# First batch's attention in two halves of 384 tokens, with a carried state column, and the order of all engine queues from a table of numbers

## The chip, the cores and the metric

The kernel runs on one core of one Trainium2 chip. The metric is the device time of one execution in microseconds (us): the median over runs is 608.11 us (three runs, 608.09 to 608.78). Engines are named as in the profile: PE (TensorE matmul), PEld (its weight load), DVE (VectorE), ACT (ScalarE), POOL (GpSimd), SP (the queue that issues the DMAs).

## What is computed

Three layers, one after another, for B = 4 batches, H = 8 heads, S = 768 tokens, D = 48 per head, so 384 channels. The first is a recurrent attention per head with a state of 48x48:

```python
f = 1.0 / (1.0 + np.exp(-f_logit))
for t in range(S):
    state = f[:, :, t, :, None] * state + np.einsum('bhd,bhe->bhde', k[:, :, t], v[:, :, t])
    y[:, :, t] = np.einsum('bhd,bhde->bhe', q[:, :, t], state)
```

Its output x (B, S, 384) goes through the second layer and that one's output through the third:

```python
theta = x @ w_theta
y = np.einsum('ts,bsd->btd', w_tok_r, x * np.cos(theta)) + np.einsum('ts,bsd->btd', w_tok_i, x * np.sin(theta))
u = x + y
x = u + np.maximum(u @ w_ch, 0.0)

h = np.maximum(x @ w_in, 0.0)
u, v = h[..., :512], h[..., 512:]
v_n = (v - mean(v)) / np.sqrt(var(v) + 1e-06)
v_s = np.einsum('ts,bsd->btd', w_spatial, v_n) + b_spatial[None, :, None]
out = (u * v_s) @ w_out
```

## The kernel before

**Stages.** Attention and second layer of all four batches form one long first part (up to about 345 us in the profile); the third layer of the four batches is the second part. In the first part PE works on the token mix of one batch (`p1_acc`, tiles `acc<-tk,z`, then `p1_h`, tiles `hh`), and the attention and angles of the next batch are laid between its matmuls. Batch 0 has no batch before it, so its attention and angles stand alone at the start of the program. That stretch is what the change rewrites.

**Attention.** The 768 tokens are 12 chunks of 64. Channels are packed densely: one dense group `g` holds 128 of the 384 channels of a batch, three groups per batch. `dense(b, g)` loads f, k, q of a group (each 128x768), forms exp and 1+exp on ACT, a running product inside each chunk on DVE (a scan, `icp<-f,one`), its log and exp on ACT (`cw`), and scales k and q on DVE (`k<-k,icp`, `icp<-cw,icp`, `cw<-icp,cw`, `q<-q,cw`). Twelve extra columns of k get the decay over a whole chunk, on POOL. In batch 0 group 0 alone is already cut in two halves of 384 tokens (`HALVES`, `cuts`). A *pair* `u` is two heads; there are four pairs a batch, and the fourth pair's channels are gathered out of the three groups by DMA into the tiles `kp` and `qp` (`att_gap`). For each pair: transposes of k (`att_k`, `pt<-ident,k`, copied by ACT to `kt`), the outer products k v of all chunks (`att_w`, `pw`, 24 matmuls), ACT copies of them and of the chunk decays, one DVE scan over 48x12 columns (`cu<-cu`, or `st`, `cb`) that turns them into the state after every chunk, the scores inside chunks (`att_s`, `psc`, 12 matmuls for six chunks, masked on DVE into `sc`), and the output (`att_x`, `px`, 46 matmuls: state times q from the second chunk on, and scores times v), copied by ACT to X.

**Second layer.** For each of six blocks of 128 tokens: transpose of X (`pt<-ident,X`), theta (`pth`), a range reduction on ACT and DVE (`sn`), two sines on ACT (another activation table than exp and log), and z = x cos, x sin on DVE. The token weights arrive as doubles, twelve parts `tok`, each turned to float32 on ACT and DVE (`tk<-ws`); a part feeds six `acc` matmuls. The theta weights (`ft<-ws`) and the channel weights w_ch (`wb<-ws`, `wc`) are converted in the same way. For batch 0 `acc`, `pth` and all attention matmuls take float32 operands, and one matmul is two rows of the trace.

**What sets the order.** Engine wrappers record every instruction of the first part (so the profile puts nearly all on one line, L496). `Plan.run` makes the order of each of the five queues (PE, DVE, ACT, POOL, SP) with a list scheduler that has a cost for each instruction, then repeats it with changed priorities drawn from the numbers in `STEPS`, and ties the instructions of each queue together in that order. POOL keeps program order, and `tables` keeps all instructions that need an activation table in program order. At the start PE runs `FILL` = 25 multiplications of the identity with itself, whose results nobody reads.

```python
self.act(f, f, AF.Exp, scale=-1.0)
A.activation(f, f, AF.Copy, bias=1.0)
V.reciprocal(fs[:, c], fc[:, :, 0])
V.memset(fc[:, :, 0:1], 0.0)
V.tensor_tensor_scan(icp, f, one, 0.0, op0=ALU.mult, op1=ALU.add)
```

Of the kernel before, what the change touches and what calls it, by code (L numbers as in the profile page):

```python
# [12 lines left out]
F32 = mybir.dt.float32  # L13
# [10 lines left out]
P = 128  # L24
# [24 lines left out]

WTICK, IDLE = 37, 25  # L50

FILL = 25

NEAR = 6
WARM = {}
# [8 lines left out]
SIGN = 0x80000000  # L64
REBIAS = 2.0**-112

MODE, HOP, ISSUE, RATE, NARROW, LAND, SLACK = 0.1, 0.11, 0.6, 310e3, 160e3, 1.2, 0.05
LEAD = 1.5  # L70
ROUNDS = 4
STEPS = [
# [11 lines left out]
]  # L84
HALVES = {0: 2}
SAMPLES, STALL, STEADY = 10, (0.07, 1.0, 3.0), 0.8
GLUE = 4
# [29 lines left out]
class Plan:  # L117
    def __init__(self, tc):
        self.tc, self.on, self.ops, self.tag, self.size = tc, True, [], {}, {}
        self.hist, self.table, self.blk, self.pri, self.gate, self.pool, self.first, self.idle = {}, None, 0, None, {}, None, {}, 0  # L120
# [4 lines left out]

    def cost(self, o, e, ins, out, src):
        n = max([b.n for b in out + src] or [0])
        k = type(ins).__name__
        if e == "A":
            if k == "InstActivation":  # L130
                return 0.19 + 0.84e-3 * n + (0.95e-3 * n if out[0].step > 2 and n > P else 0)
            return 1.28
        if e == "V":
            if o.name.startswith("tensor_tensor_scan"):
                return 0.16 + 2.07e-3 * n
            if o.name == "tensor_scalar":
                return 0.15 + 0.53e-3 * n
            if o.name == "reciprocal":
                return 0.22
            return 0.15 + 1.045e-3 * n  # L140
        if e == "G":
            return 0.1 + 0.8e-3 * n if o.name == "memset" else 0.8
        if e == "Q":
            return ISSUE
        m, r = out[0].rows, out[0].n
        o.mode = (src[-1].rows, m)
        if o.name == "transpose":
            return 0.109
        if len(src) == 2 and src[0].t == src[1].t:
            return 0.0  # L150
        if src[0].dt == F32R:
            return max(r / 2.4 + 13.3, m / 1.2 + 2) / 1e3
        if m < P:
            o.quad = (src[-1].p[0], out[0].p[0])
            return 0.064 + (0.05 if src[0].step > 1 else 0)
        return max(2 * (2 * r / 2.4 + 2), 214) / 1e3

    def add(self, e, name, ins):
# [4 lines left out]
        o.cost, o.mode = 0, None  # L163
        o.cost = self.cost(o, e, ins, o.out, o.src)
        o.bytes = max([b.n * b.rows * 4 for b in o.out] or [0])
        o.rate = RATE if max([b.rows for b in o.out] or [P]) > 96 else NARROW
# [19 lines left out]
        if e == "G":  # L186
            if self.pool is not None:
                o.dep.add(self.pool)
            self.pool = o
# [8 lines left out]
    def tables(self, o, func):  # L198
        o.func = func
        if self.table is not None:  # L200
            o.dep.add(self.table)
        self.table = o

    def prepare(self):
        ops = self.ops
        self.use, first = {}, set()
        for o in ops:
            o.new = []
            for b in o.out + o.src:
                if b.t in self.tag:  # L210
                    self.use.setdefault(b.t, set()).add(o)
                    if b.t not in first:
                        first.add(b.t)
                        o.new.append(b.t)
        self.order, self.units, self.succ, unit = {}, [], {}, {}
        for o in ops:
            for t in o.new:
                self.order.setdefault(self.tag[t], []).append(t)
# [7 lines left out]
        for u in self.units:  # L226
            mine, need = set(u), {}
            deps = {d for o in u for d in o.dep if d not in mine}
            u[0].deps = [(d, d.e == u[0].e and d.e != "Q") for d in sorted(deps, key=lambda d: d.i)]
            for o in u:  # L230
                for x in o.new:
                    need.setdefault(self.tag[x], []).append(x)
            u[0].need = list(need.items())
            for d, _ in u[0].deps:
                self.succ.setdefault(d, []).append(u)
            u[0].touch = {x for o in u for x in {b.t for b in o.out + o.src} if x in self.use}

    def schedule(self):
        free = {k: [(0.0, "")] * n for k, n in self.size.items()}
        self.took = []  # L240
        turn = {k: 0 for k in self.order}
        left = {t: len(s) for t, s in self.use.items()}
# [3 lines left out]
        for u in self.units:  # L246
            if not u[0].deps:
                insort(queue[u[0].e], (u[0].pri, u[0].i, 0.0, u))
# [1274 lines left out]
```

## Time and profile before

| | |
|---|---|
| median of three runs | 608.11 us |
| the profiled execution: its time, its span | 606.65 us, 604.9 us |
| PE busy in the span | 579.1 us (96%), 5704 matmul rows |
| DVE busy | 452.9 us (75%) |
| ACT busy | 349.3 us (58%) |
| POOL busy | 20.0 us (3%) |
| DMA, mean over the span | 230 GB/s, 139.42 MB |
| mean granted clock of PE | 0.983 |

The profiled execution is 1.75 us longer than its span (what lies around the first and last instruction) and 1.46 us shorter than the median. A granted clock of 1.00 is 2.4 GHz, one of 0.50 is 1.2 GHz; a value between is a stretch that holds both. Busy time of PE is taken from modelled ends, so a busy PE need not be PE at its peak; the distance of matmul starts tells more.

### The profile page before, as it was taken

Reading aid. Unit: us, or ns where it says so; the run is one execution under the profiler, and the core shown is the slowest. Engines: PE = TensorE matmul, PEld = TensorE weight load, DVE = VectorE, ACT = ScalarE, POOL = GpSimd, SP = SyncE. Lnnn points to the kernel's source line nnn. Section 1 sums busy time; section 2 is a strip of 40 time slices with the busy share of each in tenths; the row PEclk is TensorE's granted clock in tenths of the full one; section 3 lists DMA queues with packets and bytes.
Section 4 is the critical chain, followed back from the end, with each engine's and each line's share of the span. In section 5 each row is a group of like instructions: output and inputs, shape, how many; then the busy total and the mean of one; then the engine's idle time right before and its main releaser. Section 6 shows DMA issues by size and latency. Waiting matters only on the chain.

```text
span 604.9 us, 13976 instructions
## 1 busy us (share of the span) xinstructions
PE 579.1 (96%) x5704; PEld 533.0 (88%) x5704; DVE 452.9 (75%) x812; ACT 349.3 (58%) x649; POOL 20.0 (3%) x55
## 2 busy tenths in 40 slices
PE   7678998999999999999999999999999999999995
PEld 7675566877998999999999988999999999999995
DVE  5897899877898669857988269896668666957681
ACT  6757887478877699757973035534443454344421
POOL 3000010010010000000000000000000000000000
PEclk9589999999999999999999999999999999999998
DMA  8776779983689989667989899596029603940422
GB/s 301 226 221 221 224 251 286 322 280 124 234 280 285 314 279 298 203 214 246 298 305 317 312 313 350 199 376 233 28 93 360 231 21 110 376 154 15 138 97 84
DMA packets 65079, 139.42 MB, mean 230 GB/s; under 512 B 6128, under 2 KB 35312, under 8 KB 65008
## 3 DMA queue, kind: packets, MB, share of 16 engines
q1 hardware_dynamic: 65008, 138.45, 67.9%
q8 instruction: 47, 0.77, 0.6%
q14 instruction: 24, 0.20, 0.1%
HBM read 104.20 MB, written 31.85 MB: 225 GB/s over the span
## 4 chain that ended last, share of the span: by engine, by line
PE 80%; DMA 7%; DVE 6%; ACT 4%; issue 1%; SPq 0%; ACTq 0%; DVEq 0%
PE acc L496 24%; PE pg L496 12%; PE pu L496 8%; PE pv L496 8%; PE po L496 7%; PE hh L496 6%; PE pth L496 5%; DMA ws<-tok_dram 4%; PE psc L496 3%; PE px L496 3%; PE pw L496 2%; PE pt L496 2%; DMA xs<-x2d 1%; ACT sn L496 1%; DMA q<-qd_dram 1%
## 5 line engine op out<-in xcount | busy, mean ns | idle before, releaser
L496 PE MATMUL acc<-tk,z 128*128 128x384 f32 x792 | 172.1, 368 | 0.9 <-issue 0.9
L496 PEld LDWEIGHTS acc<-tk,z 128*128 128x128 f32 x792 | 138.0, 188 | 16.6 <-issue 0.8
L496 PE MATMUL pg<-sp,vn 128*128 128x384 f32 x504 | 88.0, 336 | 0.0
L496 PEld LDWEIGHTS pg<-sp,vn 128*128 128x128 f32 x504 | 87.4, 188 | 0.0
L496 PE MATMUL po<-wo,gt 128*128 128x384 f32 x288 | 52.1, 338 | 0.3 <-ACT gt L496 0.3
L496 PEld LDWEIGHTS po<-wo,gt 128*128 128x128 f32 x288 | 50.8, 188 | 0.8 <-ACT gt L496 0.6
L496 PE MATMUL pu<-x,wi 128*128 128x384 f32 x288 | 50.7, 335 | 0.0
L496 PEld LDWEIGHTS pu<-x,wi 128*128 128x128 f32 x288 | 50.1, 188 | 0.3
L496 PE MATMUL pv<-wi,x 128*128 128x512 f32 x216 | 50.4, 390 | 0.0
L496 PEld LDWEIGHTS pv<-wi,x 128*128 128x128 f32 x216 | 40.5, 188 | 8.1
L496 PE MATMUL hh<-uT,wc 128*128 128x384 f32 x216 | 41.7, 342 | 0.6 <-DVE uT L496 0.2
L496 PEld LDWEIGHTS hh<-uT,wc 128*128 128x128 f32 x216 | 37.9, 188 | 2.1 <-DVE uT L496 1.2
L496 ACT ACTIVATE gt<-g 128x384 fp32r<-128x384 f32 x32 | 16.7, 522 | 38.3 <-DVE g L496 38.2
L496 DVE TENSOR_TENSOR vn<-vr,vn 128x768 fp32r<-128x768 f32 x24 | 22.9, 956 | 19.8 <-ACT vn L496 19.0
L496 DVE BATCH_NORM_STATS2 st<-vr 128x6 f32<-128x512 f32 x24 | 16.4, 690 | 25.6 <-ACT vr L496 25.6
L496 PE MATMUL pth<-wh,xT 128*128 128x384 f32 x108 | 32.6, 356 | 0.0
L496 ACT ACTIVATE vn<-vr 128x768 fp32r<-128x768 f32 x24 | 20.3, 845 | 19.4 <-PE pg L496 18.8
L496 PE MATMUL psc<-qp,k 64*64 64x64 f32 x576 | 22.9, 234 | 8.1 <-ACT qp L496 6.0
L496 ACT ACTIVATE ws<-ws 128x768 f32<-128x768 f32 (+2 forms) x28 | 20.8, 741 | 16.9 <-DMA ws<-tok_dram 12.5
L496 PEld LDWEIGHTS psc<-qp,k 64*64 64x64 f32 x576 | 20.7, 147 | 9.6 <-ACT qp L496 6.4
L496 PE MATMUL px<-vc,sc 64*64 64x48 f32 x768 | 28.5, 228 | 0.0
L496 ACT ACTIVATE oo<-po 128x384 f32<-128x384 f32 x24 | 11.8, 492 | 25.5 <-PE po L496 21.3
(133 smaller groups left out, 1037.0 us busy)
## 6 DMA issues: line engine op xcount, KB each, us to landing
sp<-wpd SPq DMA_DIRECT2D x56, 576.0 KB, 6.3
tk<-tkp SPq DMA_DIRECT2D x48, 384.0 KB, 4.5
ws<-tok_dram SPq DMA_DIRECT2D x12, 768.0 KB, 6.4
tkp<-tk SPq DMA_DIRECT2D x24, 384.0 KB, 4.6
vn<-vu_dram SPq DMA_DIRECT2D x16, 288.0 KB, 4.6
vc<-va_dram SPq DMA_DIRECT2D x16, 288.0 KB, 4.7
tkd<-tk SPq DMA_DIRECT2D x12, 384.0 KB, 7.1
x2d<-xt SPq DMA_DIRECT2D x24, 192.0 KB, 3.9
```

The lines of the kernel that those rows point to most:

```text
L496: r = f(*a, **k)
```

## The change

**Halves.** In batch 0 every dense group now runs in two halves of 384 tokens (`half`), and so does everything behind it for each of the four pairs: transposes (`half_k`), gathers of the fourth pair (`half_gap`), loads of v (`half_load`), outer products and state scan (`half_w`), output (`half_x`). The program first does half 0 of all groups and pairs, then half 1. k has room for six extra columns behind each half. The state scan of a half has 48x7 columns instead of 48x12 for all: in half 0 a zero column closes each row; in half 1 the first column is the state at the end of half 0, which POOL keeps in `carry` (`carry<-cu`, `cu<-carry`). The angles of blocks 0 to 2 stand before the first dense group of batch 1, those of blocks 3 to 5 behind it. `MEMSET f` goes from DVE to POOL in every dense group. The conversion of w_ch moves from the start into the first mix (ticks `WCS` = 7, 9, 11). `FILL` is 16 instead of 25.

**Order.** The planner with its costs is gone. `LINE` gives for each engine the order of all units (a unit is one instruction; on PE one group of matmuls), 1614 numbers in all. POOL no longer has to keep program order. `tables` asks for order only between changes of the table, and `run` puts a table load in front of the exp and log instructions after each sine; the program holds 17 table loads instead of 13.

```diff
-HALVES = {0: 2}
+WCS = [7, 9, 11]
-FILL = 25
+FILL = 16
+LINE = {
+    "T": [
+        45, 61, 46, 47, 82, 48, 49, 50, 51, 52, 53, 54, 55, 56, 57, 58, 59, 60, 95, 91, 100, 120, 131, 127, 142, 136, 146, 151, 160, 156, 165, 185,
...
     def tables(self, o, func):
         o.func = func
-        if self.table is not None:
-            o.dep.add(self.table)
-        self.table = o
+        if self.table != func:
+            self.table, self.old, self.cur = func, self.cur, []
+        o.dep.update(self.old + self.cur[:1])
+        self.cur.append(o)
...
+        for e, l in LINE.items():
+            seq = [o for i in l for o in self.units[i]]
...
+                if e == "A" and o.func not in (None, func):
+                    func = o.func
+                    if func == "exp":
+                        ins.append(load().ins)
+                ins.append(o.ins)
+            for x, y in zip(ins, ins[1:]):
+                self.tc.add_manual_dep(y, x.name, no, reason="plan")
...
+    def decay(self, n, f, k, q, icp, cw, fs, cs):
+        self.act(f, f, AF.Exp, scale=-1.0)
+        A.activation(f, f, AF.Copy, bias=1.0)
+        V.reciprocal(fs, fc[:, :, 0])
+        G.memset(fc[:, :, 0:1], 0.0)
+        V.tensor_tensor_scan(icp, f, self.one[:, cs].rearrange("p c t -> p (c t)"), 0.0, op0=ALU.mult, op1=ALU.add)
...
+    def half(self, n, h):
+        for x, c in (("f", p), ("k", slice(kp.start, kp.stop - 6)), ("q", p)):
+            self.Q.dma_start(out=t[x][:, c], in_=self.a[x + "d"][n][:, p])
+        yield from self.decay(n, t["f"][:, p], k, t["q"][:, p], icp, cw, fs, slice(6 * h, 6 * h + 6))
+        if h == 0:
+            G.tensor_tensor(cx[:, 0:5], ce[:, 0:5], fs[:, 1:6], op=ALU.mult)
+            G.tensor_copy(cx[:, 5:6], ce[:, 5:6])
+        else:
+            G.tensor_copy(cx[:, 0:1], fs[:, 0:1])
+            G.tensor_tensor(cx[:, 1:6], ce[:, 0:5], fs[:, 1:6], op=ALU.mult)
...
+    def half_w(self, u, h):
+        G.memset(cu[:, 0 : 2 - h, :, 6:7], 0.0)
+        A.activation(cb[:, :, 0:6], K[:, None, TH:].to_broadcast([P, D, 6]), AF.Copy)
+        for n in range(3):
+            for s, i in ((0, 0), (1, 1), (1, 0), (0, 1)):
+                self.outer(w[s][64 * i : 64 * i + 64, n], u, 3 * h + n, s, i)
+        if h:
+            G.tensor_copy(ub[:, :, 0:1], self.carry[:, u, :, None])
+        for s in range(2):
+            A.activation(ub[:, :, h + s : h + s + 5 : 2], w[s].rearrange("p n e -> p e n"), AF.Copy)
+        V.tensor_tensor_scan(fl(cb), fl(ub), fl(cb), 0.0, op0=ALU.add, op1=ALU.mult)
+        if h == 0:
+            G.tensor_copy(self.carry[:, u, :, None], cb[:, :, 5:6])
...
+        for h in range(2):
+            for g in range(3):
+                run(self.half(g, h))
...
+                self.half_k(g, h)
+                self.half_gap(g, h)
+                if g:
+                    self.half_att(g - 1, h, X[0])
+            for u in (2, 3):
+                self.half_att(u, h, X[0])
+        run(self.p1_thetas(0, X[0], 0, 3))
+        run(self.ahead(self.dense(1, 0), 1000))
+        run(self.p1_thetas(0, X[0], 3, 6))
```

**What the order becomes, at three places.** The first is the head of the PE queue. `pt<-ident` is the fill, `pt<-ident,k_...` the transposes of a dense group's k, `pw` the outer products and `psc` the scores of pair 0. Before:

```order
L496 MATMUL pt<-ident 128x128 x25
L496 MATMUL psc<-qp_105,k_138 64x64 x12
L496 MATMUL pt<-ident,k_138 128x128 x6
L496 MATMUL psc<-qp_105,k_138 64x64 x12
L496 MATMUL pw<-vn_100,kt 64x48 x24
```

and now:

```order
L258 MATMUL pt<-ident 128x128
L258 MATMUL pt<-ident,k_137 128x128 x3
L258 MATMUL pt<-ident 128x128 x2
L258 MATMUL pt<-ident,k_203 128x128 x3
L258 MATMUL pt<-ident 128x128 x13
L258 MATMUL pw<-vn_100,kt 64x48 x12
L258 MATMUL psc<-qp_105,k_137 64x64 x12
```

Thirteen of the fills now stand behind the transposes of the second group (`k_203`) and ahead of pair 0's first outer products and scores.

The second place is DVE up to the masked scores `sc_108` of pair 0, which wait for those `psc`. Before, from the second scan of group 0 on (`k_138`, `q_141` are its k and q, `f_232` is group 1's f):

```order
L496 SCALAR_TENSOR_TENSOR icp<-f_135,one 128x384
L496 TENSOR_TENSOR k_138<-k_138,icp 128x384
L496 TENSOR_TENSOR sc_108<-psc,mask 128x384
L496 TENSOR_TENSOR icp<-cw,icp 128x384
L496 SCALAR_TENSOR_TENSOR cw<-icp,cw 128x384
L496 TENSOR_TENSOR q_141<-q_141,cw 128x384
```

and now (`f_202`, `f_296` are groups 1 and 2, `cu_249` is pair 0's state):

```order
L258 TENSOR_TENSOR q_138<-q_138,cw 128x384
L258 SCALAR_TENSOR_TENSOR icp<-f_296,one 128x384
L258 TENSOR_TENSOR icp<-cw,icp 128x384
L258 SCALAR_TENSOR_TENSOR cw<-icp,cw 128x384
L258 RECIPROCAL fs_205<-f_202 128x6
L258 TENSOR_TENSOR sc_108<-psc,mask 128x384
L258 SCALAR_TENSOR_TENSOR cu_249<-cu_249 128x336
L258 TENSOR_TENSOR q_204<-q_204,cw 128x384
```

The first halves of three groups are begun before pair 0's scores, and group 1's q and all that follows stand behind `sc_108`.

The third place is PE where the token mix begins. `ft` are the theta weights, `tk_900` and `tk_979` the first part of the token weights, `z_788` and `z_873` the first block of z, `k_748` batch 1's first k. Before:

```order
L496 MATMUL psc<-qp_105,k_748 64x64 x24
L496 MATMUL pth<-ft_171,xt 128x384
L496 MATMUL pth<-ft_178,xt 128x384
L496 MATMUL pth<-ft_185,xt 128x384
L496 MATMUL pt<-ident,X_132 128x128 x3
L496 MATMUL pth<-ft_171,xt 128x384
L496 MATMUL pth<-ft_178,xt 128x384
L496 MATMUL pth<-ft_185,xt 128x384
L496 MATMUL acc<-tk_900,z_788 128x384 x2
```

and now (`cu_738`, `cu_803` are the states of pairs 2 and 3 in half 1):

```order
L258 MATMUL px<-vc_102,sc_108 64x48 x4
L258 MATMUL psc<-qp_107,kp 64x64 x12
L258 MATMUL pth<-ft_157,xt 128x384
L258 MATMUL pth<-ft_164,xt 128x384
L258 MATMUL pth<-ft_171,xt 128x384
L258 MATMUL pw<-vn_101,kt 64x48 x12
L258 MATMUL acc<-tk_979,z_873 128x384 x2
L258 MATMUL acc<-tk_987,z_890 128x384 x2
L258 MATMUL acc<-tk_979,z_873 128x384 x2
L258 MATMUL px<-cu_803,qp_107 64x48 x4
```

Transposes, outer products and scores of batch 1's first pair (`k_748`) no longer stand ahead of the first `acc`; the last output of batch 0 (`px<-cu_803`) stands behind it.

## Rows read from the trace of the kernel before

**Rows 1.** The page: busy time by engine, and PE and its granted clock in 40 slices.

```profile
span 604.9 us, 13976 instructions
PE 579.1 (96%) x5704; PEld 533.0 (88%) x5704; DVE 452.9 (75%) x812; ACT 349.3 (58%) x649; POOL 20.0 (3%) x55
PE   7678998999999999999999999999999999999995
PEclk9589999999999999999999999999999999999998
```

**Rows 2.** Busy time by stage: stretch, its length, busy us (instructions) per engine, clock, DMA share, GB/s.

```profile
4.37:60.62 56.25, 41.99 (x939) 36.73 (x938) 46.41 (x75) 38.29 (x74) 4.51 (x15) 0.85 0.78 251
60.62:109.73 49.11, 47.08 (x593) 31.06 (x592) 44.31 (x61) 38.31 (x67) 3.17 (x6) 1.00 0.82 259
110.83:345.00 234.17, 233.22 (x2784) 219.37 (x2784) 180.24 (x269) 163.54 (x287) 8.80 (x19) 1.00 0.80 268
345.00:604.90 259.90, 252.81 (x1378) 242.29 (x1376) 180.73 (x407) 106.48 (x219) 0.00 (x0) 0.99 0.54 188
```

**Rows 3.** PE in order of time: start, length, what, count [idle before <-releaser].

```profile
1.51 5.49 PE L496 MATMUL pt<-ident 128*128 128x128 f32 x24 [1.51 <-POOL ident masks.py:199]
6.58 3.55 PE L496 MATMUL pt<-ident 128*128 128x128 f32 x27
...
24.68 1.53 PE L496 MATMUL pw<-vn,kt 64*64 64x48 f32 x48 [0.96 <-ACT kt L496]
26.00 2.42 PE L496 MATMUL psc<-qp,k 64*64 64x64 f32 x48
...
49.60 0.94 PE L496 MATMUL pw<-vn,kt 64*64 64x48 f32 x48 [0.24 <-ACT kt L496]
50.48 2.20 PE L496 MATMUL pth<-ft,xt 128*128 128x384 f32 x6
...
52.94 1.61 PE L496 MATMUL psc<-qp,k 64*64 64x64 f32 x48
...
61.31 1.45 PE L496 MATMUL acc<-tk,z 128*128 128x384 f32 x4
...
71.64 11.77 PE L496 MATMUL acc<-tk,z 128*128 128x384 f32 x36
83.25 0.82 PE L496 MATMUL pt<-ident,k 128*128 128x128 f32 x6
```

**Rows 4.** DVE in order of time: the first instructions, one of each size, and the last.

```profile
4.37 0.19 DVE L496 RECIPROCAL fs<-f 128x6 f32<-128x6 f32 x1 [0.89 <-ACT f L496]
4.73 0.96 DVE L496 TENSOR_TENSOR_SCAN icp<-f,one 128x384 f32<-128x384 f32 x1
12.45 0.56 DVE L496 SCALAR_TENSOR_TENSOR cw<-icp,cw 128x384 f32<-128x384 f32 x1
13.92 1.76 DVE L496 TENSOR_TENSOR_SCAN icp<-f,one 128x768 f32<-128x768 f32 x1
16.38 0.95 DVE L496 TENSOR_TENSOR k<-k,icp 128x768 f32<-128x768 f32 x1
17.95 1.36 DVE L496 TENSOR_TENSOR_SCAN cu<-cu 128x576 f32<-128x576 f32 x1 [0.62 <-ACT cu L496]
57.13 1.95 DVE L496 SCALAR_TENSOR_TENSOR tk<-ws,tk 128x768 uint32<-128x768 uint32 x2
59.66 0.96 DVE L496 TENSOR_TENSOR z<-sn,X 128x768 f32<-128x768 f32 x1
109.17 0.56 DVE L496 TENSOR_TENSOR uT<-xt,uT 128x384 fp32r<-128x384 f32 x1 [1.06 <-ACT uT L496]
```

**Rows 5.** The chain of waits in order of time, up to 130 us: start, length, what.

```profile
19.45 2.80 PE px L496 x92
...
30.99 4.69 DMA qp<-q
...
107.81 1.53 PE px L496 x92
109.34 1.49 PE acc L496 x4
110.83 3.15 PE hh L496 x18
```

**Rows 6.** DMA issues of the first 50 us: count, size of one, median us from issue to landing.

```profile
k<-kd_dram SPq DMA_DIRECT2D x5, 384.0 KB, 6.3
k<-kd_dram SPq DMA_DIRECT2D x2, 192.0 KB, 5.3
kp<-k SPq DMA_DIRECT2D x2, 97.5 KB, 4.7
kp<-k SPq DMA_DIRECT2D x2, 48.8 KB, 2.7
```

**Rows 7.** Busy time and clock (the last three figures: clock, DMA share, GB/s) of single stretches.

```profile
16.00:26.00 10.00, 6.69 (x188) 6.03 (x182) 9.20 (x13) 7.55 (x15) 1.08 (x3) 0.50 0.74 204
36.00:60.00 24.00, 19.43 (x484) 15.85 (x485) 18.41 (x30) 17.05 (x37) 0.49 (x3) 1.00 0.67 206
```

More of the change, by code (lines that the diff above doesn't have):

```diff
@@ L124, in tile @@
             self.tag[t.name], self.size[key] = key, bufs
[L126 to L156, printed above, removed]
     def add(self, e, name, ins):
@@ L199, in tables @@
         o.func = func
-        if self.table is not None:
-            o.dep.add(self.table)
-        self.table = o
+        if self.table != func:
+            self.table, self.old, self.cur = func, self.cur, []
+        o.dep.update(self.old + self.cur[:1])
+        self.cur.append(o)
     def prepare(self):
[L205 to L218, printed above, removed]
+        self.units, unit = [], {}
+        for o in self.ops:
             if o.e == "T" and o.blk in unit:
@@ L225, in prepare @@
             self.units.append(u)
[L226 to L236, printed above, removed]
@@ L543, in ln_exp @@
         self.ready = True
-        self.table(self.A.preload_act_table_set("natural_log_exp_and_others"), "exp")
+        if not self.plan.on:
+            self.table(self.A.preload_act_table_set(TABLES), "exp")
     def group(self):
@@ L586, in mm1 @@
             self.T.matmul(out, lhsT=l, rhs=r, start=(i == 0), stop=(i == n - 1))
-    def warm(self, p, key):
-        for _ in range(WARM.get(key, 0)):
-            self.T.matmul(p[:, 0:P], lhsT=self.ident, rhs=self.ident, start=True, stop=True)
     def att_open(self, ctx):
@@ new lines, in part, with half_k @@
+    def part(self, h):
+        return slice((TH + 6) * h, (TH + 6) * h + TH + 6)
+    def half_k(self, g, h):
+        self.group()
+        k = self.dn[g]["k"][:, self.part(h)]
+        p = self.bank("pt")
+        for i in range(3):
+            self.T.transpose(p[:, P * i : P * i + P], k[:, P * i : P * i + P], self.ident)
+        kt = self.KT[:, 0 : NT * DM].rearrange("p (n d) -> p n d", n=NT)
+        self.A.activation(kt[:, 3 * h : 3 * h + 3, P * g : P * g + P], p[:, 0:DM].rearrange("p (n d) -> p n d", n=3), AF.Copy)
@@ new lines, in half_x @@
+    def half_x(self, u, h, X):
+        self.group()
+        A, T, pr = self.A, self.T, u % NP
+        Q, sc, v, st = self.att_kq(u)[1], self.SC[u % 2], self.VC[u % 2], self.st[u, h]
+        ps = [self.bank("px")[:, 0 : 3 * D].rearrange("p (n d) -> p n d", n=3) for _ in range(2)]
+        for n in range(3 * h, 3 * h + 3):
+            four = [(c, i, ps[i][64 * (c % 2) : 64 * (c % 2) + 64, n - 3 * h]) for c in (2 * n, 2 * n + 1) for i in range(2)]
+            for c, i, o in four:
+                r = slice(64 * i, 64 * i + 64)
+                if c:
+                    T.matmul(o, lhsT=Q[r, C * c : C * c + C], rhs=st[r, c - 6 if h else c - 1], start=True, stop=False)
+            for c, i, o in four:
+                r = slice(64 * i, 64 * i + 64)
+                T.matmul(o, lhsT=sc[r, C * c : C * c + C], rhs=v[r, c], start=(c == 0), stop=True)
+        for i in range(2):
+            o = 2 * D * pr + D * i
+            A.activation(X[:, 3 * h : 3 * h + 3, o : o + D], ps[i], AF.Copy)
@@ new lines, in half_att, with outer @@
+    def half_att(self, u, h, X):
+        self.half_load(u, h)
+        if u < 3:
+            self.att_mask(u, h)
+        self.att_s(u, h)
+        self.half_w(u, h)
+        self.half_x(u, h, X)
+    def outer(self, out, u, n, s, i):
+        r = slice(64 * s, 64 * s + 64)
+        if u % NP < 3:
+            o, step = DM * n + P * (u % NP) + C * i, 1
+        else:
+            o, step = DM * n + STEP * D * i + STEP - 1, STEP
+        self.T.matmul(out, lhsT=self.KT[r, o : o + (C - 1) * step + 1 : step], rhs=self.VN[u % 2][r, i, n], start=True, stop=True)
@@ L883, in p1_tok, with p1_thetas @@
         return [x.rearrange("p (s t) -> p s t", s=2) for x in t]
-    def p1_thetas(self, b, X):
-        terms = self.p1_xt(b, X, 0)
-        for tb in range(NT):
-            nxt = self.p1_xt(b, X, tb + 1) if tb + 1 < NT else None
+    def p1_thetas(self, b, X, first=0, last=NT):
+        terms = self.p1_xt(b, X, first)
+        for tb in range(first, last):
+            nxt = self.p1_xt(b, X, tb + 1) if tb + 1 < last else None
             self.p1_z(b, X, tb, self.p1_theta(b, tb, terms))
@@ L1416, in run @@
         self.mixes(X, sa, sw, se)
-        self.plan.run()
+        self.plan.run(lambda: self.A.preload_act_table_set(TABLES))
+        self.last, self.ready = self.plan.end, False
         self.ln_exp()
```

448 lines of the change are left out of this document (96 added, 352 removed), and 77 rows, old and new, of tables (LINE, STEPS).

## Prediction

> **What bounds the kernel now.** I read the page first [rows 1]: PE is busy in 96% of the span, its slices (15 us each) are nearly full from the fifth on, and the granted clock falls below 0.9 in the second and third alone. So the question is where PE does not yet run full. The busy times by stage [rows 2] answer it. From 110.83 to 345.00 us PE is busy 233.22 of 234.17 us, so what a new order can take out of the long middle is about 1 us; the last stretch, 259.9 us, is outside the table. What is left is the start. PE in order of time [rows 3] shows the first token-mix matmul (`acc`) at 61.31 us: until then batch 0's attention runs alone, as a chain PE, ACT, DVE, PE. DVE is the busiest engine beside PE there: 46.41 of 56.25 us up to the first z and 44.31 of 49.11 us from there to the third uT, the operand of the first `hh` [rows 2, 4], which starts at 110.83 [rows 5]. Its idle time is 9.8 and 4.8 us, 14.6 together. So up to 110 us DVE's queue sets the pace, and I account for the change on DVE, then test the result against PE.
>
> **DVE up to the first z.** Sizes from [rows 4]: products 0.56 (384 columns) or 0.95 (768), product scans 0.96 or 1.76, state scan 1.36 (576 columns), two steps of a token part 1.95. A state scan of 336 columns has no row; from 0.96 and 1.76 a column costs 0.8/384 = 2.1 ns, so it takes 0.86, between 0.79 (336/576 of 1.36) and 0.96. Reciprocals, memsets and the one-step conversions of 0.36 or 0.56 come from the same view. In the order of the program, before: scans 2x0.96 + 3x1.76 = 7.2; state scans 4x1.36 = 5.4; score masks 10x0.56 = 5.6; products 8x0.56 + 12x0.95 = 15.9; theta weights 4.4; channel weights 5.6; one token part 2.5; the rest 3.1; together 49.7. Now: scans 6x0.96 + 1.76 = 7.5; state scans 7x0.86 = 6.0; masks 7x0.56 = 3.9; products 24x0.56 = 13.4; theta weights 4.4; two token parts 4.9; the rest 3.7; together 43.9. The channel weights and most of batch 1's first group are no longer ahead of z, a second token part and two angles are.
>
> **DVE from there to the third uT.** Before 47.3: seven token parts 17.2, five z 4.8, eight products 7.6, scans 3.5, state scans 4.1, the rest 10.1. Now 56.1: five token parts 12.3, five z 4.8, twelve products 11.4, scans 5.3, state scans 4.9, the postponed channel weights 5.6, the rest 11.8. Over both pieces: 96.9 before, 100.0 now. Halves cost 3.1 us of DVE, since every cut instruction pays its fixed part twice; `MEMSET f`, 0.07 each, is the only thing taken off. The record shows 46.4 + 44.3 = 90.7 busy for the 96.9, because neighbours overlap: a factor of 0.94. The 3.1 becomes 2.9.
>
> **The sum.** DVE begins at 4.37 in both, since both begin with the same half of group 0. Let X be DVE's idle time up to the third uT: 14.6 before. The first `hh` then comes 14.6 - 2.9 - X = 11.7 - X earlier. PE is also a little further on at that point: before, it has done 44 `acc` matmuls, now 42; 36 trace rows in 11.77 us, two to a matmul, make that 1.3 us less [rows 3]. But outer products and scores of batch 1's fourth pair are done, 0.94 + 1.61 = 2.5 us [rows 3]. So 1.2 us is won beside, and the gain is **12.9 - X**.
>
> **X, in three parts.** (a) DVE's `sc_108` waits for the scores behind thirteen fills. By the durations above DVE reaches k of group 1 at 4.37 + 4.3 = 8.7; three transposes at half clock take 0.8 (six at full clock 0.82 [rows 3]), so the 26 fill rows start at 9.5. The fill before runs 24 rows in 5.49 us at first and 27 in 3.55 us later [rows 3], 0.22 and 0.13 us apart: 5.7 or 3.3 us. With half of a pair's outer products and scores (1.53 and 2.42, or 0.94 and 1.61 for a whole one [rows 3]) the scores are there at 17.2 or 14.1. DVE has done all it may do ahead of them at 8.7 + 3.4 = 12.1. The wait is 5.0 or 2.0; I take 3.8, nearer the slow one, as PE has done little before. ACT stands behind the same `pw`, so nothing covers it. (b) Other waits up to the first z: between 0 and the 9.8 of before. The new order puts work of another group or pair between the steps of each half, and a walk through the queues with the rows' durations finds each product there just in time; I take 2.0. (c) From z to uT: between 0 and the 4.8 of before; I take 3.0, since the queue is longer and PE asks earlier. X = 8.8, gain 4.1.
>
> **Beside DVE.** PE: the first `acc` comes at 4.37 + 0.94x43.9 + 5.8 = 51.4 instead of 61.31. From there to the first `hh` lie 42 `acc` matmuls (27.5), three thetas (6.6), 27 transposes (3.7), four pairs' products (3.8) and scores (6.4) and three and a half outputs (5.4), 53.4 us by [rows 3, 5]: PE could be at `hh` by 104.8, DVE lets it at about 107.9, so PE waits some 3 us in this stretch and does not decide. ACT has some 43 us of work up to the first z, as much as DVE, and four table loads more in all; it is busy 38.3 of 56.3 us now [rows 2], and I give it no term of its own beside (b). SP: 28 DMAs more, about half a us each, on a queue that mostly waits. The transfers move the same bytes; a half of k lands 5.3 us after issue where a whole one takes 6.3 [rows 6], so halves come little sooner, but they are issued in the order of need and the first f is the same. The gathers of the fourth pair (4.69 us on the chain for `qp` now [rows 5]) become 16 of 48.8 KB or less; the nearest row has 2.7 us at that size [rows 6], and they are needed later than that after issue. The Trainium skill, DMA: Bandwidth & Descriptors, section Rules for kernel authors, speaks against such cuts: many small transfers should be coalesced, under 64 KB one mostly pays overhead. The rows half agree (half the bytes save 1.0 us of 6.3); by the rule alone a half gather would take as long as a whole one, 4.7 us, which would still end ahead of its use. Fill: nine fewer cost nothing. POOL: the first column of f is now zeroed there, between a reciprocal and a scan; the order has another DVE instruction between them nearly everywhere. After 110 us DVE has 77% load [rows 2] and the same work left as before, so I expect the gain to stay.
>
> The profiled execution is 606.65 us, 604.9 of it span, and 1.46 below the median. 4.1 less is 602.5 for a profiled execution, and 608.1 - 4.1 = **604.0 us** for the median. A measurement can tell about 0.2% (1.2 us) from no change.
>
> **Rivals.**
> - *DVE fed without gaps.* (a) at 2.0, (b) 0.5, (c) 2.0: X = 4.5, gain 8.4, **599.7 us**. For it: DVE holds 9.20 busy in the 10 us from 16 on even now [rows 7]. Against it: in-order queues with five engines waiting for each other, and PE, too, must then do its 53.4 us ahead of `hh` without a gap. Chance 0.15.
> - *The gaps only change their place.* Eight chains of transposes, products, scan and output instead of four, each with the same hops, X about 12.5: **608 us**, no gain. For it: the gaps of before are also such hops. Chance 0.15.
> - *PE at half clock up to the mix: slower.* The clock is 0.50 from 16 to 26 us, where PE runs in pieces, and 1.00 from 36 on, after the work of three pairs had come together [rows 7]. At 1.2 GHz a pair costs 0.81 (scores) + 1.27 (output, 2.80 against 1.53) + 0.59 (products) = 2.7 us more [rows 3, 5], four pairs 10.7; three thetas of 2.2, doubled, 6.6 more. The new order spreads this work thinner, half a pair at a time, so all 17 us could be paid, half of it where DVE waits. X = 8.8 + 8.5 = 17.3, gain -4.4, **612.5 us**. It decides from X = 12.9 on. Against it: the chain has other halves between its steps, and before already pays the half clock for two pairs. The Trainium skill, TensorE: Matmul & The Clock Gate, section What's actually happening, states the rule by which this would happen: 1.2 GHz is the state of rest, and only recent activity lifts it. The rows agree, 0.50 in the thin stretch and 1.00 in the full one. Chance 0.16.
>
> **Numbers.** Forecast (X between 6 and 11.5, 601.2 to 606.7) 0.54; the rivals 0.15, 0.15, 0.16. Faster: 0.54 + 0.15 + 0.04 of the second rival = 0.73. Same: 0.09 of the second and 0.01 of the third = 0.10. Slower: the rest, 0.17. The range runs from 598.5 (X = 3.3, little but the fast fill's 2.0 left of it) to 609.5 (X = 14.3, about what it is before); it leaves out most of the third rival and a little at the lower end, some 0.2.
>
> **What would show it.** Right: first `acc` near 51 us, first `hh` near 108, with PE idle for some 3 us between them; a gap of 2 to 5 us on DVE ahead of the first score mask; DVE idle some 9 us up to uT; nothing changed from 345 us before the end on. Wrong: first `acc` later than 56 us; PE's clock at 0.50 up to the mix; DVE waiting on gathers or on POOL; or PE no longer full between `hh` and the second part, so that what was won is given back.

## The result: 0.9% slower

The changed kernel takes 612.17 us (median of 12 runs, 609.47 to 614.26) where the kernel before took 607.51 in the same job (12 runs, 604.02 to 610.00): a ratio of 1.0091, 95% interval 1.0072 to 1.0111. A second measurement gave 1.0100 (1.0066 to 1.0134). The profiled execution is 613.34 us, 611.6 of it span, 6.7 us of span more than before.

The page of the changed kernel, beside [rows 1]: PE's row of slices has a dip in the 24th slice that was not there (351.7 to 367.0 us), the clock's row one in the 25th, and in the list of groups `pv` has got an idle time of 5.8 us.

```profile
span 611.6 us, 14051 instructions
...
PE 580.7 (95%) x5686; PEld 532.2 (87%) x5686; DVE 454.0 (74%) x815; ACT 355.4 (58%) x683; POOL 31.9 (5%) x95
...
PE   5699999999999999999999959999999999999994
...
PEclk9789999999999999999999998999999999999998
...
L258 PE MATMUL pv<-wi,x 128*128 128x512 f32 x216 | 53.5, 406 | 5.8 <-DVE xt L258 5.8
```

Busy times by stage of the changed kernel, in the columns of [rows 2]. The first three lines answer to the first three there: up to the first z DVE idles 46.56 - 39.71 = 6.9 us (9.8 before), from there to the first `hh` 3.1 us (4.8), and after that PE is nearly as full as before, 236.71 of 238.92 us (233.22 of 234.17). The other three are the hand-over from the mix to the second part, where PE is busy 8.2 of 14 us and the clock falls to 0.62.

```profile
4.44:51.00 46.56, 37.21 (x754) 31.80 (x755) 39.71 (x72) 34.79 (x88) 13.84 (x48) 0.85 0.72 221
51.00:106.08 55.08, 54.71 (x863) 37.81 (x862) 51.96 (x75) 48.98 (x90) 4.32 (x13) 1.00 0.79 279
106.08:345.00 238.92, 236.71 (x2719) 221.89 (x2718) 180.79 (x265) 162.90 (x286) 11.32 (x22) 1.00 0.81 272
...
356.00:362.00 6.00, 2.98 (x15) 2.25 (x13) 5.90 (x12) 2.94 (x5) 0.00 (x0) 1.00 0.61 235
362.00:370.00 8.00, 5.26 (x12) 4.13 (x13) 4.56 (x14) 3.50 (x6) 0.00 (x0) 0.62 0.64 228
370.00:380.00 10.00, 10.00 (x46) 8.58 (x45) 2.88 (x13) 1.86 (x6) 0.00 (x0) 0.96 1.03 301
```

PE in order of time there, first of the kernel before, then of the changed one (columns as in [rows 3]).

```profile
358.92 1.85 PE L496 MATMUL hh<-uT,wc 128*128 128x384 f32 x9 [0.19 <-DVE xt L496]
360.61 12.44 PE L496 MATMUL pv<-wi,x 128*128 128x512 f32 x54
372.89 12.67 PE L496 MATMUL pu<-x,wi 128*128 128x384 f32 x72
```

```profile
355.05 1.85 PE L258 MATMUL hh<-uT,wc 128*128 128x384 f32 x9 [0.25 <-DVE xt L258]
356.75 2.24 PE L258 MATMUL pv<-wi,x 128*128 128x512 f32 x9
364.74 13.32 PE L258 MATMUL pv<-wi,x 128*128 128x512 f32 x45 [5.75 <-DVE xt L258]
377.90 12.67 PE L258 MATMUL pu<-x,wi 128*128 128x384 f32 x72
390.40 9.86 PE L258 MATMUL pg<-sp,vn 128*128 128x384 f32 x56
```

The changed kernel begins `pv`, the second part's first product, 3.86 us earlier than before. It computes one token tile (nine matmuls) and waits; the other 45 matmuls then take 13.16 us to the first `pu`, 292 ns each, where before 54 took 12.28, 227 ns each. DVE shows what PE waits for: the last two `xt<-hh` of the mix, which in the kernel before follow their `hh` at once (360.31 and 361.24), now stand behind the conversions of the spatial weights and of `wo`.

```profile
358.31 0.55 DVE L496 SCALAR_TENSOR_TENSOR xt<-hh,xt 128x384 f32<-128x384 f32 x1
...
360.31 0.55 DVE L496 SCALAR_TENSOR_TENSOR xt<-hh,xt 128x384 f32<-128x384 f32 x1
360.78 0.55 DVE L496 TENSOR_TENSOR wo<-wb,wo 128x384 fp32r<-128x384 f32 x1
361.24 0.55 DVE L496 SCALAR_TENSOR_TENSOR xt<-hh,xt 128x384 f32<-128x384 f32 x1
```

```profile
354.45 0.55 DVE L258 SCALAR_TENSOR_TENSOR xt<-hh,xt 128x384 f32<-128x384 f32 x1
...
356.96 0.35 DVE L258 TENSOR_SCALAR wb<-ws 128x384 uint32<-128x384 uint32 x1
...
361.46 0.55 DVE L258 SCALAR_TENSOR_TENSOR xt<-hh,xt 128x384 f32<-128x384 f32 x1
...
363.65 0.56 DVE L258 TENSOR_TENSOR wo<-wb,wo 128x384 fp32r<-128x384 f32 x1 [0.59 <-ACT wo L258]
364.13 0.55 DVE L258 SCALAR_TENSOR_TENSOR xt<-hh,xt 128x384 f32<-128x384 f32 x1
...
376.39 0.27 DVE L258 TENSOR_REDUCE gs<-gc 1x1 f32<-1x128 f32 x1 [8.14 <-DMA gc<-gr]
```

`pv` does not read `xt`. But PE's products land in PSUM, a memory of eight banks; the mix's pool there has tiles for all eight (3 `acc`, 3 `att`, 2 `th`), and the second part's pool takes the same eight: a `pv` tile in the bank of an `hh` must wait until `xt<-hh` has read it. The first tile found a free bank, the second did not.

### The profile page after: what moved, and what is told of

It reads as the page before. It is cut to its first block, busy times and chain, and to the rows that moved or that the text cites. A ratio compares the mean times of both kernels' runs of the same rounds, so it can differ in the third digit from the quotient of the medians.

```text
span 611.6 us, 14051 instructions
## 1 busy us (share of the span) xinstructions
PE 580.7 (95%) x5686; PEld 532.2 (87%) x5686; DVE 454.0 (74%) x815; ACT 355.4 (58%) x683; POOL 31.9 (5%) x95
## 5 line engine op out<-in xcount | busy, mean ns | idle before, releaser
L258 PE MATMUL pv<-wi,x 128*128 128x512 f32 x216 | 53.5, 406 | 5.8 <-DVE xt L258 5.8
L258 PEld LDWEIGHTS pv<-wi,x 128*128 128x128 f32 x216 | 42.4, 197 | 15.0 <-DVE xt L258 6.2
L258 ACT ACTIVATE sn<-sn 128x384 f32<-128x384 f32 x48 | 24.9, 520 | 5.1 <-DVE sn L258 4.7
L258 PEld LDWEIGHTS px<-vc,sc 64*64 64x64 f32 x768 | 25.5, 144 | 0.1
```

Of the source, the lines that this page charges most:

```text
L258: r = f(*a, **k)
```

## The account by stages

Every kernel of the study, by the first matmul of each name on PE in its profiled execution. In the second part `pv` and `pu` are the two halves of x @ w_in, `pg` is the spatial product of the weights `sp` with the normalised `vn`, and `po` the last product of `wo` with the gated `gt`. The columns: the first `acc`; the first `pv`; from there to the first `pg`; from there to the start of the last `po`; from there to the end of the span. Medians are compared by the ratio to the kernel before of the same job.

| kernel | median us (runs) | ratio (95%) | acc | pv | pv to pg | pg to last po | end |
|---|---|---|---|---|---|---|---|
| before | 607.51 (12) | | 61.31 | 360.61 | 24.79 | 212.91 | 6.56 |
| the change | 612.17 (12) | 1.0091 (1.0072-1.0111) | 52.45 | 356.75 | 33.66 | 212.40 | 8.83 |
| e1_last_xt | 605.03 (12) | 0.9968 (0.9946-0.9990) | 52.79 | 357.91 | 24.77 | 212.70 | 9.02 |
| e2_pv_again | 613.88 (4) | 1.0113 (1.0062-1.0163) | 53.60 | 358.04 | 30.89 | 213.74 | 9.14 |
| e3_fills_first | 606.73 (10) | 1.0006 (0.9977-1.0034) | 50.32 | 354.56 | 28.71 | 214.61 | 9.25 |
| e4_xt_and_flag | 602.60 (12) | 0.9936 (0.9911-0.9960) | 52.49 | 355.75 | 24.79 | 212.54 | 7.24 |
| e5_after_again | 612.71 (6) | 1.0100 (1.0066-1.0134) | 52.88 | 356.62 | 32.31 | 212.41 | 9.35 |
| e6_before_late_xt | 612.36 (4) | 1.0105 (1.0059-1.0151) | 60.45 | 359.76 | 31.19 | 212.82 | 6.82 |
| e7_all_three | 601.42 (6) | 0.9906 (0.9874-0.9938) | 49.05 | 355.20 | 24.77 | 212.42 | 7.15 |
| e8_table_load_early | 599.32 (6) | 0.9877 (0.9840-0.9914) | 49.71 | 353.95 | 24.79 | 212.95 | 7.15 |
| e9_flag_alone | 610.03 (9) | 1.0068 (1.0040-1.0097) | 52.52 | 356.71 | 33.65 | 212.46 | 7.24 |
| e10_xt_split_bs | 602.81 (9) | 0.9931 (0.9898-0.9963) | 53.77 | 359.14 | 24.77 | 212.42 | 7.53 |
| e11_pv_again_flag | 616.31 (6) | 1.0159 (1.0126-1.0192) | 52.46 | 356.59 | 33.00 | 217.91 | 7.48 |
| e12_again_late_flag | 611.68 (9) | 1.0067 (1.0038-1.0096) | 52.59 | 358.19 | 30.89 | 212.58 | 9.53 |
| e13_late_flag | 612.33 (6) | 1.0091 (1.0059-1.0122) | 51.92 | 353.59 | 32.41 | 212.60 | 9.96 |
| e14_best_late_flag | 602.42 (7) | 0.9920 (0.9891-0.9949) | 49.12 | 351.15 | 24.77 | 213.77 | 9.81 |

For the change the columns add up: -3.86 up to `pv`, +8.87 from `pv` to `pg`, -0.51 from there to the last `po`, +2.27 at the end, together +6.77. The 8.87 are 5.94 of wait (364.74 - 356.75 less 2.05 for nine matmuls at 227 ns) and 2.93 of slow rows (13.16 less 45 x 0.2274). How far single executions scatter: `pv` begins between 355.8 and 359.1 in nine of the ten kernels that have the change's fills, and at 353.6 in the tenth, e13_late_flag. What part of the 3.86 us up to `pv` comes from the halves and what part from the new order, no run here separates.

## Experiments

**The place of the last xt<-hh.** e1_last_xt moves two units in DVE's table and nothing else:

```
-1514, 1568, 1569, 1575, 1602, 1603, 1604, 1571, 1606, 1583, 1609, 1579, 1521, 1610, 1611, 1613, 1528,
+1514, 1568, 1569, 1521, 1575, 1528, 1602, 1603, 1604, 1571, 1606, 1583, 1609, 1579, 1610, 1611, 1613,
```

> Only DVE's table is edited: the last two xt<-hh units stand 2 and 4 places earlier-placed work ahead, so that each runs right after its hh matmuls instead of behind the conversions of wt, X, wb and wo. Theory (the wait of the second pv tile for the last xt<-hh costs 5.75 us and the slow clock behind it some 3 us): pv x54 without a gap in about 12.3 us from about 356.8, the granted clock 1.00 there, pg starts near 381.5 instead of 390.40, and the run comes to about 603.3 us against 612.2 for the change and 607.5 for the kernel before. Rival A (the hand-over is paced by DVE and ACT, which stood still for 8.1 us until gc<-gr landed at 376.39): pv starts on time, but the first pg waits for vn until about 384 to 386, and the run comes to 606 to 608. Rival B (the second pv tile waits for other work): no change, 612.

PE of e1_last_xt:

```profile
357.91 12.43 PE L258 MATMUL pv<-wi,x 128*128 128x512 f32 x54
370.18 12.67 PE L258 MATMUL pu<-x,wi 128*128 128x384 f32 x72
382.68 17.49 PE L258 MATMUL pg<-sp,vn 128*128 128x384 f32 x100
```

The gap and the slow rows are gone, 24.77 us from `pv` to `pg` as before the change. The ratio falls from 1.0091 to 0.9968, 1.2% or 7.5 us: the change's loss at the hand-over was the place of two entries in a table. Rival B falls; of rival A nothing shows, `pg` follows `pu` at once. The median is 605.0 and not 603.3; the profile shows as much: against the change the stage is 8.9 us shorter, but `pv` began 1.2 us later in this execution, and what lies behind the first `pg` is 0.5 us longer.

e6_before_late_xt is the converse: in the kernel before, the last `xt<-hh` goes to the end of DVE's part of the plan, behind the last `wo` conversion.

```
 seq = self.refine(best)
+v = seq["V"]
+x = [o for o in v if o.name == "scalar_tensor_tensor" and o.out[0].t.startswith("xt")][-1]
+v.remove(x)
+v.append(x)
```

> The kernel before with one DVE instruction moved: the last xt<-hh of the mix stands behind the last wo conversion, as it does in the change's table; all that the planner ordered before it stays. Theory (it is this place in DVE's queue that lost the time): the second pv tile waits from about 362.9 until the last wo conversion is over at about 369.4 and xt behind it, some 7 us, the clock falls and the rest of pv takes 3 us longer, so 8 to 10 us over the kernel before, 614 to 617. Rival (the loss belongs to the halves or to the carried states): within 2 us of the kernel before.

```profile
359.76 4.29 PE L500 MATMUL pv<-wi,x 128*128 128x512 f32 x18
368.54 10.06 PE L500 MATMUL pv<-wi,x 128*128 128x512 f32 x36 [4.49 <-DVE xt L500]
378.44 12.67 PE L500 MATMUL pu<-x,wi 128*128 128x384 f32 x72
```

A ratio of 1.0105, some 6 us: the same wait with the same slow rows behind it, in a kernel without halves and without a table. It is less than the 8 to 10 expected: the third `pv` tile waited, not the second, and the last conversion was over at 368.0 instead of 369.4.

**The slow rows.** e2_pv_again keeps PE busy through the wait:

```
-self.mm3(p, [(x2[0][:, j, sl], x2[1][:, j, sl], wi[0][:, j, FF:], wi[1][:, j, FF:]) for j in range(NJ)])
+for _ in range(4 if again and s == 0 else 1):
+    self.mm3(p, [(x2[0][:, j, sl], x2[1][:, j, sl], wi[0][:, j, FF:], wi[1][:, j, FF:]) for j in range(NJ)])
...
-            run(self.p2_v())
+            run(self.p2_v(b == 0))
```

> The nine matmuls of the first pv tile of the first batch are computed four times into the same tile, so that PE stays busy through the 5.75 us in which it waited; the order of the work is that of the change. It separates the wait from the clock. Theory (the rows of pv after the gap took 296 ns instead of 227 because PE had idled and was granted half the clock): the 45 rows after the wait take 10.2 us instead of 13.3, granted clock 1.00, the run about 609.2 us, 3.0 under the change. Rival (the rows were slow for the stores and loads that run at the same time): the rows stay slow, the run is at 612 or longer.

From `pv` to `pg` it takes 30.89 us, as the theory had it, but its median is no better than the change's. DVE stands still there 9.6 us for `gc<-gr`, a step of the flag: DVE compares the tile `ge` with a limit (`gt`) and reduces it to one value a partition (`gr`), a DMA moves these 128 values into one row (`gc`), and DVE takes their minimum (`gs`), which the branch at the end of the program reads. So it was tried again with the flag moved (below), and then with the flag truly out of the way.

> The edit of e2_pv_again (the first pv tile computed four times) on top of e9_flag_alone, since the saving of 2.8 us that the stage showed in e2_pv_again could not be seen in its total. Theory: from the first pv to the first pg 30.9 us as in e2_pv_again against 33.65 in e9_flag_alone, the clock at 1.00 throughout, and the run 2.8 us under e9_flag_alone, about 607.2, ratio to the kernel before about 1.002. Rival (what the faster rows save is lost again in the second part, where e2_pv_again took 213.7 us from the first pg to the last po against 212.4): 609.5 to 610.5, ratio about 1.006, and again a wait of po for gt.

```profile
389.59 3.39 PE L258 MATMUL pg<-sp,vn 128*128 128x384 f32 x18 [1.47 <-ACT u L258]
```

```profile
386.01 0.27 DVE L258 TENSOR_REDUCE gs<-gc 1x1 f32<-1x128 f32 x1 [12.06 <-DMA gc<-gr]
```

Both theories missed. The rows ran at full speed, but DVE stood still 12.1 us for `gc<-gr`, a transfer of half a KB; ACT stood behind DVE, and `pg` and `po` waited for `u`, `vn` and `gt`. Moving the call had not put the flag later: the compile-time scheduler still issued `gt` and `gr` right behind the plan, and what moved was `gc<-gr`, behind eight loads of `sp` on SP's queue. In e12_again_late_flag and e13_late_flag one more line ties `gt` to the last `vn` of the first batch:

```
+i = V.tensor_scalar(t, self.ge.rearrange("p u c -> p (u c)"), LIMIT, None, op0=ALU.is_le)
+self.tc.add_manual_dep(i.ins, self.end[1], mybir.DependencyInfo(mybir.DependencyClass.NoSync, mybir.DependencyReason.DATA), reason="order")
```

> The first pv tile computed four times as in e2_pv_again, and the flag ordered behind the last vn of the first batch, so that gc<-gr (for which DVE stood still 9.6 us in e2_pv_again and 12.1 us in e11_pv_again_flag) is out of the hand-over. If the clock alone costs what the stage shows: from the first pv to the first pg 30.9 us or less, no wait of pg, from there to the last po 212.4 to 213, and the run 2.5 to 3 us under e13_late_flag. If DVE and ACT still cannot follow: pg waits for vn or u, and the run is at or above e13_late_flag.

> The change with the flag alone ordered behind the last vn of the first batch. If the wait of DVE and ACT for gc<-gr (8.1 us in the change) costs nothing there, because PE has its own 5.75 us of wait and slow rows: pv to pg 33.6 us as in the change, and the run at 610 to 612 (the length of the end decides within that). If it costs: 2 us or more shorter from pv to pg.

PE of e12_again_late_flag:

```profile
358.19 18.55 PE L258 MATMUL pv<-wi,x 128*128 128x512 f32 x81
376.57 12.67 PE L258 MATMUL pu<-x,wi 128*128 128x384 f32 x72
```

81 matmuls in 18.38 us, 227 ns each; nothing waits later. The 27 extra matmuls (6.1 us) outlast e13_late_flag's wait (5.4 us) by 0.7, and the clock saves 2.2 there, so the stage takes 30.89 against 32.41 us. The medians are 611.68 and 612.33, and their intervals overlap: in the total the clock's part could not be told. Without `gc<-gr` the change stays where it was (1.0091, and 32.41 us from `pv` to `pg` beside 33.66 and 32.31 in the two runs of the change): no cost of it shows there, where PE has a wait of its own.

The clock after gaps of different length, each over the rest of `pv` after the wait (in e3_fills_first after a second one of 0.34 us):

| gap on PE | kernel | matmuls, us | ns each | granted clock |
|---|---|---|---|---|
| 5.75 | the change | 45, 13.16 | 292 | 0.77 |
| 5.67 | e9_flag_alone | 45, 13.22 | 294 | 0.77 |
| 5.23 | e5_after_again | 45, 12.34 | 274 | 0.83 |
| 5.22 | e13_late_flag | 45, 12.46 | 277 | 0.82 |
| 4.49 | e6_before_late_xt | 36, 9.90 | 275 | 0.83 |
| 2.98 | e3_fills_first | 36, 8.29 | 230 | 1.00 |
| none | e12_again_late_flag | 81, 18.38 | 227 | 1.00 |

Beyond the 24.79 us of the kernel before, the stage lost 1.4 to 1.6 times the waits of 4.49 to 5.75 us, and 3.92 us for the two waits of e3_fills_first, 3.32 together.

**The fills ahead.** e3_fills_first moves thirteen fill matmuls in PE's table:

```
-45, 61, 46, 47, 82, 48, 49, 50, 51, 52, 53, 54, 55, 56, 57, 58, 59, 60, 95,
+45, 46, 47, 48, 49, 50, 51, 52, 53, 54, 55, 56, 57, 58, 59, 60, 61, 82, 95,
```

> Only PE's table is edited: the 16 fill matmuls all stand at the front, none between the transposes of the second pair's k and the first pw. Theory of the prediction (DVE's idle time from 12.34 to 15.52 is the wait behind 13 fills): that gap shrinks from 3.18 us to under 1, the first acc moves from 52.45 to about 50, and the run is 2 to 3 us under the change, about 609.5. Rival (the clock): PE idles before the first pw, is granted half the clock for longer, and the gap only changes place: first acc at 52 or later, the run at 612 or longer.

The change's start of this stretch (PE, then DVE), then that of e3_fills_first with its hand-over (PE, then the last two `xt<-hh` on DVE):

```profile
10.02 4.19 PE L258 MATMUL pt<-ident 128*128 128x128 f32 x26
14.14 0.56 PE L258 MATMUL pw<-vn,kt 64*64 64x48 f32 x24
```

```profile
15.52 0.56 DVE L258 TENSOR_TENSOR sc<-psc,mask 128x384 f32<-128x384 f32 x1 [3.18 <-PE psc L258]
```

```profile
2.17 5.84 PE L258 MATMUL pt<-ident 128*128 128x128 f32 x32 [2.17 <-POOL ident masks.py:199]
...
10.23 0.56 PE L258 MATMUL pw<-vn,kt 64*64 64x48 f32 x24
...
354.56 2.25 PE L258 MATMUL pv<-wi,x 128*128 128x512 f32 x9
359.80 2.34 PE L258 MATMUL pv<-wi,x 128*128 128x512 f32 x9 [2.98 <-DVE xt L258]
```

```profile
359.19 0.55 DVE L258 SCALAR_TENSOR_TENSOR xt<-hh,xt 128x384 f32<-128x384 f32 x1
...
361.87 0.55 DVE L258 SCALAR_TENSOR_TENSOR xt<-hh,xt 128x384 f32<-128x384 f32 x1
```

The gap on DVE is gone, the first `acc` comes at 50.32 instead of 52.45, and `pv` begins 2.2 us earlier; the rival falls. Over the kernels of the table, the four with the fills in front begin `acc` at 49.55 and `pv` at 353.72 us in the mean, the ten with the change's fills at 52.75 and 356.93: the wait behind the fills, 3.18 us, was real and passed through whole. The run gains more than that, 0.85% or 5.2 us. The last `xt<-hh` ends 7.9 us behind the start of `pv` as in the change, but here the second `pv` tile waited for the earlier of the two, so that PE idled 2.98 and 0.34 us instead of 5.75, and the clock held: 5.0 us less from `pv` to `pg`. Of these 2.2 were lost again behind `pg` (214.61 against 212.40), where `po` waits 1.96 us for `gt`.

**The end.** e4_xt_and_flag adds to e1_last_xt:

```
-        self.flag(self.d1, bad)
...
+            if b == 0:
+                self.flag(self.d1, bad)
             if b + 1 < B:
```

> The edit of e1_last_xt, and the flag (gt, gr, gc, gs, bad) is computed in the second stage of the first batch instead of ahead of it, so that DVE and ACT no longer stand still for gc<-gr. If theory holds for e1_last_xt and pg is not held up there: the same as e1_last_xt, about 603.3 us. If rival A holds there: 603 to 604 here, and e1_last_xt 3 to 4 us above it.

602.6 us, ratio 0.9936. But from `pv` to `pg` nothing is won against e1_last_xt (24.79 against 24.77), and DVE still waits for `gc<-gr`, 2.7 us and later. What is shorter is the end, 7.24 us instead of 9.02, and the way to `pv`, by 2.2 us, within the scatter above. Two runs look at the end:

> The change with the flag moved into the second stage of the first batch, and nothing else. It tells what the flag costs where the change has it. So far the stretch from the last matmul's start to the end of the span took 8.8 to 9.4 us in the kernels that have the flag there and 7.2 us in the three that have it moved. Theory (the flag's place costs only this end): pv in two pieces as in the change, pg near 390, the end 7.2 us, the run 610 to 611. Rival (gc<-gr, for which DVE and ACT wait 8.1 us, also holds up the hand-over): pg 3 us or more earlier, the run at 608 or less. Third (the end's length is chance): 8.8 to 9.4 us again and 612.

> The edit of e1_last_xt, and the load of bs split into two of half its size, which adds one instruction to SP's queue and leaves the flag where the change has it. If the end of 9.0 us of e1_last_xt comes from the flag's place: 9 us again, the time of e1_last_xt, 604 to 606. If it comes from where the instructions of SP's queue happen to lie: 7.2 us or another length, and 602 to 604. The split itself costs under 1 us on SP's queue, ahead of gc<-gr.

```
-self.Q.dma_start(out=self.bs, in_=self.a["bs"].partition_broadcast(P))
+for h in range(2):
+    sl = slice(TH * h, TH * h + TH)
+    self.Q.dma_start(out=self.bs[:, sl], in_=self.a["bs"][sl].partition_broadcast(P))
```

The waits of SP's queue in the last microseconds, of the change and of e10_xt_split_bs (engine, line, what it waited for, us in total, times, the longest):

```profile
SPq L1270 <- SPq L1270: 4.6, 2, 2.7
```

```profile
SPq L1272 <- SPq L1272: 3.0, 1, 3.0
```

After the branch at the end of the program SP walks through a row of semaphores. In the change it stops a second time there, 1.85 us, for no transfer of the kernel and no engine that the trace names; so it does in e1_last_xt, e2_pv_again, e3_fills_first, e5_after_again, e12_again_late_flag, e13_late_flag and e14_best_late_flag (1.85 to 2.36), and not in the other seven nor before. One more instruction on SP, with the flag left where it was, takes it away (end 7.53), and e12_again_late_flag to e14_best_late_flag have the stop with the flag moved: the flag's place alone does not decide it. Ratios: 1.0091 to 1.0068 for e9_flag_alone, 0.9968 to 0.9931 for e10_xt_split_bs, whose intervals each overlap with those of their partners. The Trainium skill, Runtime: NRT & Kernel Launch, section Instruction fetch mechanics, says that instructions come in blocks through a DMA queue of the engine, and that a taken branch whose target isn't loaded stops it until the block is fetched. The traces agree as far as they go: within each of the eight stops two packets of 8 KB run on the queue that the page of the profile lists as `q14 instruction`, the later of them ends 1.0 to 1.2 us before the stop does, and behind the branch that queue moves 6 packets in these eight kernels, 4 or 5 in the other eight. So a fetch goes with every stop. That the place of the instructions decides whether it is needed is argued here and not shown.

**The better version.** e7_all_three puts e4_xt_and_flag and the fills together; e8_table_load_early also moves the ACT_TABLE_LOAD at the hand-over behind the last sin.

```
+            final = [None, *(o for o in seq if o.func == "sin")][-1]
...
+                if o is final:
+                    ins.append(load().ins)
...
-        self.last, self.ready = self.plan.end, False
+        self.last, self.ready = self.plan.end, True
```

> The edits of e1_last_xt, e3_fills_first and the moved flag together. If the gains add: e4_xt_and_flag less the 2.2 us by which e3_fills_first began pv earlier, about 600.4 us, 1.0% under the kernel before. Rival (the time won ahead is lost again at the hand-over, where DVE and ACT have their own work to finish): 602 to 603, and pu or pg waits for vr or vn.

> The kernel of e7_all_three, with the ACT_TABLE_LOAD that stood between the plan's last ACT instruction and the first vr<-pv moved behind the last sin of the plan. Theory (ACT has slack at the hand-over once pv flows): the time of e7_all_three within 0.2%. Rival (the 1.28 us of the load delay vr and with it pg): 1 us or more under e7_all_three.

> The kernel of e8_table_load_early with the flag ordered behind the last vn of the first batch instead of behind eight loads of sp. PE already takes 24.79 us from pv to pg there, as in the kernel before, so all theories expect the time of e8_table_load_early within 0.3%, 598 to 601 us.

601.42 and 599.32 us, 0.9906 and 0.9877: both beat both kernels, e8_table_load_early by 1.2% (0.9 to 1.6) the kernel before. The gains of e7_all_three add up, about 1 us short of the 600.4 us expected. Whether the table load does anything is not settled: the intervals overlap, and from `pv` to `pg` both take what PE needs, 24.8 us. e14_best_late_flag is no faster, 602.42; its end is 2.7 us longer, the stop of SP again.

The control, the changed kernel once more, came out as it should, 1.0% above the kernel before with a gap of 5.23 us, and rows of 274 ns:

> The changed kernel itself once more, beside the kernels of this job and the same runs of the kernel before. All theories: 0.7 to 1.1% above the kernel before, pv in two pieces with 5 to 6 us between, and rows of some 300 ns behind it at half the clock.

## Why the prediction was wrong

- *"From 110.83 to 345.00 us ... the last stretch, 259.9 us, is outside the table", and "nothing changed from 345 us before the end on".* This step failed. The first part does not end at about 345 us, as the description of the kernel has it, but with the last `hh` of the mix at 360.8. The table does not name the second part's instructions, but it orders DVE's and ACT's last instructions of the mix, and these run up to 364.7 us, across the seam. Their order decides when PSUM banks come free for the second part. The cost was 8.9 us from `pv` to `pg`; [rows 2] has only a sum for that stretch. The order on DVE after 345 us could be read before the run; I looked at the table's start alone. Another 2.3 us came at the end of the program (8.83 against 6.56), 1.85 of them the second stop of SP, which no term and no rival had; why the change has it stays open.
- *"DVE has 77% load ... and the same work left as before, so I expect the gain to stay".* Same error: a mean load over 234 us says nothing of the last 20, where `xt<-hh` came some 7 us after its `hh`, behind conversions on a full queue (5.90 of 6.00 busy).
- *Gain 12.9 - X with X = 8.8.* The size came out, in part by luck. First `acc` 52.45 (expected 51.4). First `hh` 4.0 us earlier, 106.40 against 110.37 by PE's order of time (the chain of [rows 5] has it from 110.83); `pv` 3.86 earlier; expected 4.1. But DVE idles 6.85 + 3.12 = 10.0 us instead of 8.8 by these stretches, and is busy 91.7 after 90.7 [rows 2], where 2.9 more was expected; with the next item these are three errors of 1 to 2 us that nearly cancel. e4_xt_and_flag and e10_xt_split_bs, which have neither the wait nor the stop, are 0.6 and 0.7% under the kernel before, some 4 us: there the gain that was forecast is seen in the total.
- *The 1.2 us that PE would be further on at the first `hh`.* Not seen: 3.97 us won there, 3.86 at `pv`.
- *(a) Wait behind thirteen fills, 2.0 to 5.0, taken 3.8.* 3.18 us, and all of it came back in the mean of the kernels that have the fills in front.
- *PE idle 3 us ahead of `hh`, since DVE's queue sets the pace up to there.* Wrong for the second stretch: PE is busy 54.71 of 55.08 us from 51 us on. The last operands of the first `hh` were ready at 105.45 (`uT`) and 105.92 (`wc`), and PE came to it from its own `acc` matmuls at 106.40. From `acc` to `hh` it took 53.95 us, as PE's own list in the prediction has it (53.4).
- *Rival, slower by the clock up to the mix.* The half clock was there, 0.50 from 28 to 36 us in the change, but the mean up to the first z was 0.85, as before [rows 2], and the first `acc` came at 52.45. That its 612.5 us is near the measured 612.17 is chance. The clock fell later, behind the wait at the hand-over, after PE had been busy 2.98 of 6.00 us: 0.77 over 13.2 us. The Trainium skill, TensorE: Matmul & The Clock Gate, section What's actually happening, says that a PE that has done little falls back to 1.2 GHz; the trace agrees at that place.
- *Rivals in general.* The slower case was looked for in the stretch that the change is about. None of the rivals asked what the new order ends with, and the sign nearest to it, PE no longer full between `hh` and the second part, stops where the loss begins.

## To carry over

When an order table is replaced, read its end as closely as its start: on each engine the last instructions before the seam, and what the next stage needs from them beside data, above all PSUM banks and buffers. Here the instruction that frees a bank had to go first, small as it is; the conversions ahead of it were for products that began over 20 us later (`pg` at 390.40, `po` at 412.25). And when a gain of 4 us meets a loss of 9, undoing one entry of the table shows in one run whether the idea or its schedule lost.

## What the runs showed that was not expected

A wait on PE of 4.5 to 5.75 us was followed by rows at 274 to 294 ns instead of 227, at a mean granted clock of 0.77 to 0.83 between the levels 1.2 and 2.4 GHz; after 2.98 us it stayed at 1.00. A transfer of half a KB took 3.6 us to land in the kernel before and 9.8 in e11_pv_again_flag behind eight loads of 576 KB, and everything behind it on DVE's queue waited with it. And with one more instruction on SP the end of a program was 1.5 us shorter.
